# Strassen products of the first layer: from the first halves of batches 3, 5 and 7 to four tiles of batch 1

## The chip, the cores and the metric

The kernel runs on one core of a Trainium2 chip. The core has a matrix engine (TensorE, PE), a vector engine (VectorE, DVE), a scalar engine (ScalarE, ACT), a general engine (GpSimd, POOL), and a queue engine (SyncE, SP) that issues most of the transfers. They share an on-chip memory (SBUF); PE writes its results into a small accumulator memory (PSUM), from which DVE and ACT read. The metric is the device time of one execution in microseconds (us). The kernel before has a median of 765.96 us over three runs (765.54 to 766.06).

## What is computed

An attention block that reads a small state, followed by a two-layer network whose weights are shared by all tokens:

```python
def _attn_ref(x, state):                      # x: 8 x 8 x 512 x 64, state: 8 x 8 x 32 x 64
    scale = 1.0 / np.sqrt(D)
    scores = scale * np.matmul(x, state.transpose(0, 1, 3, 2))
    a = softmax(scores)
    xread = np.matmul(a, state)
    scores2 = scale * np.matmul(state, x.transpose(0, 1, 3, 2))
    a2 = softmax(scores2)
    sread = np.matmul(a2, x)
    return np.concatenate([xread, sread], axis=2)

def _moe_ref(x, w_in, w_out):                 # x: 4352 x 512, d_ff 2048
    h = x @ w_in
    g = h * np.cos(h)
    return g @ w_out
```

(`softmax` stands here for the three lines of the reference that subtract the maximum, exponentiate and divide by the sum.) There are 8 batches of 512 token rows and 32 state rows. All is computed in float32; the weights arrive as float64 and are converted on the chip.

## The kernel before

**The first layer through the state.** A token's row is a mean of state rows with attention weights, so the kernel doesn't form the row. It multiplies the state with `w_in` once for each batch (`products`, kept in `sw`), and then the attention weights `aT` (256 of them for each token, in two groups of 128 partitions) with `sw`. A batch has 2048 hidden columns, worked on as 16 *tiles* of 128 columns by 512 tokens. A *plain* tile is two matmuls of 512 columns into a PSUM buffer (`hidden`, line 471). There are two such buffers (`hps`), used in turn.

**Strassen couples.** For some tiles, two neighbouring tiles are computed together: a 2 x 2 block product (two groups of state rows by two tiles, two groups by two halves of the tokens) with 7 half-width products in place of 8. `hidden_a` issues four of the products (L514), `hidden_b` three. They need:
- four differences of the attention weights for each batch (`halves`, L493, on DVE, kept in `aS`);
- four sums of 128 x 128 blocks of `sw` for each couple (`sw_sums`, L509): on POOL, except that line 506 puts them on DVE where `t.b < 2 or t.b == 2 and t.f == 0`;
- an ACT copy of one product to SBUF (L536), and five sums on DVE (`sums_a`: L544, L545, L546; `sums_b`: L559, L560) that make the two tiles in `g_all`, in SBUF, before the gate.

Where a plain tile stands directly ahead of a Strassen couple, its result is first copied out of PSUM by ACT (L957), since the couple takes both PSUM buffers.

**The gate.** `h cos h` is four operations for each tile: ACT rounds (L567, `gate`), DVE subtracts (L570, `gate2`), ACT takes the sine (L573, `gate3`), DVE multiplies (L580, `gate4`). For a plain tile L570 and L580 read `h` in PSUM; for a tile of a couple they read it in SBUF, in `g_all`.

**The second layer by Strassen.** Batches are paired (0 and 1, 2 and 3, ...). A pair's 32 tiles go through four phases of 8 tiles. In phases 2 and 3 (the odd batch) differences of gated tiles are formed (`minus`, L586): on POOL, except that in the later pairs one for each tile is on DVE. Products of the second layer (L624) follow three steps behind the tile; two of the seven products of a pair are done in the next pair's steps (`more`).

**The order.** The schedule is written out by hand, and each engine runs its queue in that order. A *step* is one tile; step 16 b + f is tile f of batch b. `plan` spreads the attention of the next batch over the steps: DVE transposes (L301), scores on PE (L319), maxima, exponentials on ACT, sums and norms (L333 to L386). During batches 0 and 1 the weights are also converted (L228, L231 on ACT, L234, L237 on DVE, L242 on POOL, up to step 16), and at steps 16 to 22, and 32 and 33, POOL forms the sums of blocks of `w_out` that the second layer's Strassen needs (`blocks`, L912). Within a step the order is: the step's first-layer matmuls and, ahead of a couple, that couple's first four products; attention on PE; gate and subtraction; the couple's sums; attention on DVE; the sine; a store; state sums for a couple two steps on; the product; `minus`; attention again; differences of attention weights for a couple five steps on; POOL's block sums; the second layer's matmuls.

**Which tiles are in couples.** `seven(t)` on line 480 decides. Before, these are all 16 tiles of batches 2, 4 and 6 (phases 0 and 1) and the first 8 of batches 3, 5 and 7 (phase 2). `halves` of an odd batch is issued in the last couple of the even one, that of an even batch five steps ahead of it (L1009).

Of the kernel before, what the change touches and what calls it, by code (L numbers as in the profile page):

```python
# [21 lines left out]
def kernel(  # L22
# [44 lines left out]
    NH = NF // 2  # L67
# [75 lines left out]
    def states(half, to):  # L143
        for i in range(4):
            nc.tensor.transpose(out=to[:, P * i:P * i + P],
                                in_=st[:, 4 * half + i, :], identity=ident)
# [36 lines left out]
    def fetch(n):  # L183
        nonlocal n_fetched
        while n_fetched < n:
            dst, src = loads[n_fetched]
            if f64:
                m, w = dst.shape[1:]

                at_, c0 = (n_fetched - 2) % 3, 0  # L190
                if n_fetched < 4:
                    at_, c0 = n_fetched // 2, n_fetched % 2 * 2 * m * w
                if n_fetched >= N_LOADS:
                    at_ = 3 + n_fetched - N_LOADS
                raw = raw_at[at_].bitcast(I32)[:, c0:c0 + 2 * m * w]
                raw = raw.rearrange("p (m f) -> p m f", m=m)
                nc.sync.dma_start(out=raw, in_=src.bitcast(I32))
                raws[n_fetched] = raw.rearrange("p m (f w) -> p m f w", w=2)
            else:
                nc.sync.dma_start(out=dst, in_=src)  # L200
            n_fetched += 1
# [6 lines left out]
    def convert(i, parts):  # L208

        for p in parts:
            if p == "f":
                if i not in (1, 2) and i + 3 < N_LOADS:
                    fetch(max(i + 4, 6))
            elif f64:
                convert_part(i, p)
# [234 lines left out]
    def part(b, name, *args):  # L453

        if b not in attn:
            attn[b] = Attention(b)
        getattr(attn[b], name)(*args)
        if (name, args) == ("reads", (1,)) and b + 1 < B:
            if b > 0:
                attn[b + 1] = Attention(b + 1)  # L460
                attn[b + 1].load_tokens()
            load_x(b + 1)
# [5 lines left out]
    def hidden(t):  # L468
        t.hp = hps.tile([P, S], F32, name="h")[:, 0:t.n]
        for i in range(t.kn):  # L470
            nc.tensor.matmul(out=t.hp, lhsT=t.lhs(i), rhs=t.rhs(i),  # L471
                             start=(i == 0), stop=(i == t.kn - 1))
# [4 lines left out]


    def seven(t):
        return t.pair is not None and t.b > 1 and t.phase < 3  # L480

    def new_pair(t):
        return t.b % 2 == 0 and t.f == 0

    def halves(b):
        aT = aT_of[b]
        b11, b12 = aT[:, 0, 0:HS], aT[:, 0, HS:S]
        b21, b22 = aT[:, 1, 0:HS], aT[:, 1, HS:S]  # L490
        for i, x1, x2 in ((0, b12, b11), (1, b22, aS[:, 0]), (2, b22, b12),
                          (3, b21, aS[:, 1])):
            nc.vector.tensor_tensor(aS[:, i], x1, x2, op=ALU.subtract)  # L493
# [22 lines left out]
    def take_slot(t):  # L516
        t.slot = g_free.pop(0)
        t.hp = t.g = g_all[:, t.slot, 0:t.n]
# [7 lines left out]
    def hidden_a(t, t2):  # L526
        b11, b12, b21, b22 = blocks_of(t)
        t.h1, t.h2 = [hps.tile([P, S], F32, name="h") for _ in range(2)]
        product_of(t.h1[:, LO], b11, aT_of[t.b][:, 0, LO])
        product_of(t.h1[:, HI], swS[:, 1], aS[:, 1])  # L530
        product_of(t.h2[:, HI], b21, aS[:, 2])
        product_of(t.h2[:, LO], swS[:, 0], aS[:, 0])
        take_slot(t)
        take_slot(t2)
        t.second = t2
        nc.scalar.copy(t.g[:, LO], t.h1[:, LO])  # L536
# [12 lines left out]
    def hidden_b(t):  # L549
        b11, b12, b21, b22 = blocks_of(t)  # L550
        t.h1, t.h2 = [hps.tile([P, S], F32, name="h") for _ in range(2)]
        product_of(t.h1[:, LO], b12, aT_of[t.b][:, 1, LO])
        product_of(t.h2[:, HI], swS[:, 2], aT_of[t.b][:, 1, HI])
        product_of(t.h2[:, LO], b22, aS[:, 3])

    def sums_b(t):
        e, o = 2 * t.slot, 2 * t.second.slot
        add = nc.vector.tensor_tensor
        add(t.g[:, LO], t.g[:, LO], t.h1[:, LO], op=ALU.add)  # L559
        add(both(o, e + 1), both(o, e + 1),  # L560
            t.h2.rearrange("p (h s) -> p h s", h=2), op=ALU.add)
# [3 lines left out]
    def gate(t):  # L565
        t.q = msb.tile([P, S], F32, name="q")[:, 0:t.n]
        nc.scalar.activation(t.q.bitcast(I32), t.hp, func=ACTF.Copy, bias=0.25)  # L567

    def gate2(t):
        nc.vector.tensor_tensor(t.q, t.q.bitcast(I32), t.hp, op=ALU.subtract)  # L570

    def gate3(t):
        nc.scalar.activation(t.q, t.q, func=ACTF.Sin, bias=halfpi,  # L573
                             scale=-TWO_PI)

    def gate4(t):
        if not hasattr(t, "slot"):
            t.slot = g_free.pop(0)
            t.g = g_all[:, t.slot, 0:t.n]
        nc.vector.tensor_tensor(t.g, t.hp, t.q, op=ALU.mult)  # L580
# [217 lines left out]
    def warm(n, to):  # L798

        for _ in range(n):  # L800
            nc.tensor.matmul(out=to, lhsT=zeros[:, 0:P], rhs=zeros, start=True,
                             stop=True)
# [124 lines left out]
    for step, t in enumerate(all_tiles):  # L927
        s = step % NF
        if s == 0 and t.b < B:
            steps = plan(t.b)  # L930
        todo = [p[s] if t.b < B else [] for p in steps]

        def go(n):
            for p in todo[n]:
                part(*p)

        last, conv = conv_at.get(step - 1, -1), conv_at.get(step, -1)
        if step == B * NF + (0 if f64 else 8):
            fetch(N_LOADS + 2)
        if step == 4:  # L940
            warm(1, acc[MAIN][0])
        ahead = all_tiles[step + 1:step + 3]
        if seven(t):
            if t.f % 2 == 0:
                hidden_b(t)
                sums_b(t)
                if s == NF - 2 and seven(all_tiles[step + 2]):
                    halves(t.b + 1)
        elif step != 1:
            hidden(t)  # L950
        first = len(ahead) > 1 and seven(ahead[0]) and ahead[0].f % 2 == 0
        if first:
            if not seven(t):

                h = t.hp
                take_slot(t)
                nc.scalar.copy(t.g, h)  # L957
            hidden_a(*ahead)
        if step == 0:
            hidden(all_tiles[1])  # L960
            warm(3, acc[MAIN][0])
            gate(t)
            gate2(t)
            convert(3, "bcdf")
            convert(4, "1")
            go(0)
        else:
            go(0)
            if step == 5:
                states(1, acc[SIDE][1])  # L970
            if not (seven(t) and t.f % 2):
                gate(t)
            gate2(t)
            if step == 3:
                warm(4, acc[MAIN][0])
                part(0, "products", 1, SIDE)
            if first:
                sums_a(ahead[0])
            go(1)
            go(3)  # L980
            if step == 1:
                convert(4, "bcdf")
            elif last >= 0:
                convert(last, "bcdf")
            if conv >= 0 and not todo[1]:
                convert(conv, "1")
        gate3(t)
        if seven(t) and t.f % 2 == 0:
            gate(t.second)
        if step == 3:  # L990
            part(0, "products_kept", 1, SIDE)
        if later:
            later.pop(0)()
        for u, new in zip(all_tiles[step + 2:step + 4], (False, True)):
            if seven(u) and u.f % 2 == 0 and new_pair(u) == new:
                sw_sums(u)
        gate4(t)
        if conv >= 0 and todo[1] and step > 0:
            convert(conv, "1")
        if t.pair is not None:  # L1000
            sums(t)
        if step == 6:
            states_kept(1, acc[SIDE][1])
        go(2)
        if conv >= 0:
            convert(conv, "2")
        go(4)
        for u in all_tiles[step + 5:step + 6]:
            if seven(u) and new_pair(u):  # L1009
                halves(u.b)  # L1010
        if step in block_at:
            blocks(*block_at[step])
        if t.pair is not None:
            sums2(t)
        while len(line) >= (LAG if step >= 2 * NH else LAG + 1):
            output(line.pop(0))
        line.append(t)
# [32 lines left out]
```

## Time and profile before

| what | value |
|---|---|
| median of three runs | 765.96 us |
| the profiled execution | 765.96 us |
| its span, first to last instruction | 764.2 us |
| granted PE clock | 0.997 |
| PE busy | 751.7 us, 2880 records |
| DVE busy | 520.3 us, 862 instructions |
| ACT busy | 316.3 us, 523 instructions |
| POOL busy | 249.3 us, 258 instructions |
| PE busy, 0 to 75 us | 68.64 us |
| PE busy, 75 to 160 us | 85.00 us |
| PE busy, 160 to 764 us | 598.09 us |
| DVE busy, 94 to 131 us (batch 0's last steps and the first half of batch 1) | 29.26 of 37 us |
| POOL busy, 94 to 131 us | 28.44 of 37 us |

A float32 matmul shows as two records. A group's mean is the length of one record from its start to its modelled end; successive records overlap, so the distance from one start to the next is what a record adds to PE's time. In rows of the timeline the columns are the start, the length, the engine, the line, the operation, what is written and read, the shape, the count, and in brackets the idle time ahead of it with what ended it. Busy time doesn't tell whether an operation was working or held up: where another engine stands in its way inside the operation, the row is simply longer than others of its form.

In the built program the tiles of batch 1 begin at 97.48 us (step 16) and step 24 begins at 130.43; the first couple of batch 2 is issued at 168.89.

### The profile page before, as it was taken

To read this page: it belongs to the slowest core of one execution; us is meant where nothing else is said; L and a number is where in the kernel's file an instruction comes from. 1 tells how busy PE (TensorE), PEld (TensorE's weight loads), DVE (VectorE), ACT (ScalarE), POOL (GpSimd) and SP (SyncE) were. 2 spreads that over 40 slices of the span, in tenths; PEclk is the share of its full clock that TensorE was granted. 3 is DMA by queue.
4 is the path that set the end of the run, shared out by engine and by line. 5 is a ranking of instruction groups with operands and counts; after the bars stand their busy time and mean duration, and the time that the engine had idled before them with its cause. 6 is when DMAs were issued, how large, how long until landed. Compare 5 with 4: busy or idle time off the path is not lost.

```text
span 764.2 us, 8416 instructions
## 1 busy us (share of the span) xinstructions
PE 751.7 (98%) x2880; PEld 380.4 (50%) x2880; DVE 520.3 (68%) x862; ACT 316.3 (41%) x523; POOL 249.3 (33%) x258
## 2 busy tenths in 40 slices
PE   8998999999999999999999999999999999999997
PEld 3443443445555554445555553445555554455554
DVE  5778777836896788847886789747878676432431
ACT  3887844533254335333362335333443333212212
POOL 2354278777121210662221111751211206500200
PEclk9999999999999999999999999999999999999999
DMA  8595461050002510340105210420100115000021
GB/s 247 170 274 209 131 98 29 4 107 1 14 15 49 90 28 4 54 82 0 29 1 97 41 28 15 70 54 1 27 1 1 28 28 138 0 0 15 14 42 41
DMA packets 161962, 43.54 MB, mean 57 GB/s; under 512 B 153920, under 2 KB 153920, under 8 KB 161920
## 3 DMA queue, kind: packets, MB, share of 16 engines
q1 hardware_dynamic: 161024, 42.49, 25.7%
q10 hardware_dynamic: 768, 0.39, 0.2%
q8 instruction: 23, 0.38, 0.2%
q14 instruction: 19, 0.16, 0.1%
q0 software_dynamic: 128, 0.13, 0.1%
HBM read 34.08 MB, written 8.91 MB: 56 GB/s over the span
## 4 chain that ended last, share of the span: by engine, by line
PE 87%; DVE 7%; ACT 2%; issue 1%; DMA 1%; POOL 1%; SPq 0%; DVEq 0%; ACTq 0%; POOLq 0%
PE o L624 47%; PE h L514 14%; PE h L471 14%; PE at L319 4%; PE o L744 4%; PE at L409 2%; DVE xT L339 1%; PE o L319 1%; DVE q L570 1%; DVE g_all L580 1%; DVE i L333 1%; DMA g_all<-in_moe_w_in_dram 1%; ACT q L567 1%; PE at L392 1%; DVE aT L356 1%
## 5 line engine op out<-in xcount | busy, mean ns | idle before, releaser
L624 PE MATMUL o<-g_all,w_out 128*128 128x512 f32 x512 | 236.4, 598 | 0.4 <-POOL w_out L242 0.4
L624 PE MATMUL o<-g_all,s 128*128 128x512 f32 x384 | 177.3, 598 | 0.0
L586 POOL TENSOR_TENSOR g_all<-g_all 128x512 f32<-128x512 f32 x80 | 112.8, 1433 | 121.2 <-DVE g_all L580 121.2
L624 PEld LDWEIGHTS o<-g_all,w_out 128*128 128x128 f32 x512 | 93.8, 190 | 113.1 <-issue 108.4
L573 ACT ACTIVATE q<-q,halfpi 128x512 f32<-128x512 f32 (+1 forms) x144 | 100.8, 700 | 95.8 <-DVE q L570 95.6
L624 PEld LDWEIGHTS o<-g_all,s 128*128 128x128 f32 x384 | 70.8, 190 | 88.1 <-issue 82.1
L570 DVE TENSOR_TENSOR q<-q,h 128x512 f32<-128x512 int32 (+1 forms) x69 | 42.9, 621 | 103.6 <-ACT q L567 103.6
L471 PE MATMUL h<-aT,sw 128*128 128x512 f32 x224 | 107.2, 602 | 4.8 <-DVE g_all L580 4.3
L567 ACT ACTIVATE q<-g_all 128x512 int32<-128x512 f32 x75 | 46.8, 624 | 141.8 <-DVE g_all L560 141.4
L567 ACT ACTIVATE q<-h 128x512 int32<-128x512 f32 (+1 forms) x69 | 37.6, 545 | 131.0 <-PE h L471 131.0
L570 DVE TENSOR_TENSOR q<-q,g_all 128x512 f32<-128x512 int32 x75 | 52.7, 703 | 35.5 <-ACT q L567 35.5
L471 PEld LDWEIGHTS h<-aT,sw 128*128 128x128 f32 x224 | 41.8, 190 | 60.2 <-issue 45.0
L509 POOL TENSOR_TENSOR swS<-sw 128x128 f32<-128x128 f32 x35 | 17.4, 496 | 148.6 <-PE h L514 107.3
L580 DVE TENSOR_TENSOR g_all<-g_all,q 128x512 f32<-128x512 f32 x75 | 54.0, 720 | 14.5 <-ACT q L573 14.4
L580 DVE TENSOR_TENSOR g_all<-h,q 128x512 f32<-128x512 f32 (+1 forms) x69 | 42.8, 621 | 23.5 <-ACT q L573 23.1
L242 POOL TENSOR_TENSOR w_out<-w_out,s 128x1024 int32<-128x1024 int32 x10 | 23.9, 2390 | 77.6 <-DVE w_out L237 73.4
L509 POOL TENSOR_TENSOR swS<-sw,swS 128x128 f32<-128x128 f32 x35 | 18.3, 522 | 87.4 <-PE h L514 86.9
L514 PEld LDWEIGHTS h<-aT,sw 128*128 128x128 f32 x144 | 27.4, 190 | 34.4 <-issue 28.0
L514 PE MATMUL h<-aS,sw 128*128 128x256 f32 x144 | 43.1, 381 | 0.1
L514 PE MATMUL h<-aS,swS 128*128 128x256 f32 x144 | 42.8, 379 | 0.0
L514 PE MATMUL h<-aT,sw 128*128 128x256 f32 x144 | 42.8, 379 | 0.0
L586 DVE TENSOR_TENSOR g_all<-g_all 128x512 f32<-128x512 f32 x48 | 33.5, 697 | 1.6
(107 smaller groups left out, 886.3 us busy)
## 6 DMA issues: line engine op xcount, KB each, us to landing
out_dram<-ot SPq DMA_DIRECT2D x132, 64.0 KB, 2.0
g_all<-in_moe_w_out_dram SPq DMA_DIRECT2D x8, 1024.0 KB, 5.0
g_all<-in_moe_w_in_dram SPq DMA_DIRECT2D x6, 1024.0 KB, 5.3
xT<-in_x_dram SPq DMA_DIRECT2D x96, 64.0 KB, 2.3
x_b<-in_x_dram SPq DMA_DIRECT2D x24, 256.0 KB, 4.5
x_b<-in_x_dram SPq DMA_DIRECT2D x16, 128.0 KB, 3.8
g_all<-in_moe_w_in_dram SPq DMA_DIRECT2D x4, 512.0 KB, 5.9
x_b<-in_moe_w_out_dram SPq DMA_DIRECT2D x1, 1024.0 KB, 6.1
```

The lines of the kernel that those rows point to most:

```text
L242: nc.gpsimd.tensor_tensor(bits, bits, e, op=ALU.add)
L319: nc.tensor.matmul(out=(to or at)[j][Ns * k:Ns * k + Ns, 0:n], lhsT=w[D * j:D * j + D, self.b, Ns * k:Ns * k + Ns], rhs=r(slice(D * j, D * ...
L471: nc.tensor.matmul(out=t.hp, lhsT=t.lhs(i), rhs=t.rhs(i), start=(i == 0), stop=(i == t.kn - 1))
L509: engine.tensor_tensor(o, x1, x2, op=op)
L514: nc.tensor.matmul(out=out, lhsT=w, rhs=r, start=True, stop=True)
L567: nc.scalar.activation(t.q.bitcast(I32), t.hp, func=ACTF.Copy, bias=0.25)
L570: nc.vector.tensor_tensor(t.q, t.q.bitcast(I32), t.hp, op=ALU.subtract)
L573: nc.scalar.activation(t.q, t.q, func=ACTF.Sin, bias=halfpi, scale=-TWO_PI)
L580: nc.vector.tensor_tensor(t.g, t.hp, t.q, op=ALU.mult)
L586: engine.tensor_tensor(out, a, b, op=ALU.subtract)
L624: nc.tensor.matmul(out=acc[bank][ch], lhsT=w[:, i, P * ch:P * ch + P], rhs=g.g, start=(i == 0), stop=(i == NH - 1))
L744: nc.tensor.matmul(out=acc[MAIN][i], lhsT=t.g[:, P * i:P * i + P], rhs=w_out[:, :, t.f, :], start=(t.n_th == 0), stop=(t.n_th == NF - 1))
```

## The change

`seven` takes another set of tiles: tiles 4 to 7 of batch 1 (two couples) come in, and the first halves of batches 3, 5 and 7 (12 couples) go out and are plain again. Batches 2, 4 and 6 stay. The second edit issues `halves(1)` five steps ahead of tile 4 of batch 1, that is at step 15; the `halves` of batches 3, 5 and 7 are no longer issued.

```diff
     def seven(t):
-        return t.pair is not None and t.b > 1 and t.phase < 3
+        if t.b == 1:
+            return 4 <= t.f < NH
+        return t.pair is not None and t.b > 1 and t.phase < 2
@@
         for u in all_tiles[step + 5:step + 6]:
-            if seven(u) and new_pair(u):
+            if seven(u) and new_pair(u) or (u.b, u.f) == (1, 4):
                 halves(u.b)
```

What follows from it in the queues, with the lines as they are numbered before: the couples of batch 1 are tiles 20 and 21, and 22 and 23. `hidden_a` of the first is issued in step 19, behind the plain tile 19, whose result ACT copies out (L957); `hidden_a` of the second in step 21. Their state sums are issued in steps 18 and 20 ahead of that step's product (L580), on DVE by line 506, which is as it was. In the built programs PE has 40 full-width matmuls more (L471) and 70 half-width ones fewer (L514); DVE has 8 fewer L493, 8 more L509 and 50 fewer of the couples' sums; ACT has 10 fewer L536 and one more L957; POOL has 48 fewer L509. 19 tiles more have their L567, L570 and L580 read PSUM. SP's queue is the same in both.

## The prediction

> **What bounds the kernel now.** I read the page first (busy shares, then the chain that ended last), then that chain in order of time, then the timelines of TensorE (PE), VectorE (DVE), ScalarE (ACT) and GpSimd (POOL) over the steps that change. From the page, shares of the span, the chain and three groups:
>
> ```profile
> PE 751.7 (98%) x2880; PEld 380.4 (50%) x2880; DVE 520.3 (68%) x862; ACT 316.3 (41%) x523; POOL 249.3 (33%) x258
> PE 87%; DVE 7%; ACT 2%; issue 1%; DMA 1%; POOL 1%; SPq 0%; DVEq 0%; ACTq 0%; POOLq 0%
> L471 PE MATMUL h<-aT,sw 128*128 128x512 f32 x224 | 107.2, 602 | 4.8 <-DVE g_all L580 4.3
> L514 PE MATMUL h<-aS,sw 128*128 128x256 f32 x144 | 43.1, 381 | 0.1
> L586 POOL TENSOR_TENSOR g_all<-g_all 128x512 f32<-128x512 f32 x80 | 112.8, 1433 | 121.2 <-DVE g_all L580 121.2
> ```
>
> PE is busy 98% and carries 87% of the chain, so its arithmetic is the time, unless another engine makes it wait. The means in the groups (602, 381 ns) overlap, so I price a record by the chain in order of time (start, length, number of records):
>
> ```profile
> 334.84 1.72 PE h L471 x4
> 187.13 3.43 PE o L624 x8
> 190.57 1.73 PE h L514 x8
> ```
>
> A 512-column record costs 1.72/4 = 0.43 us, a 256-column one 1.73/8 = 0.216. Every matmul is two records.
>
> **PE's arithmetic.** A couple of plain tiles is 4 matmuls, 8 records at 0.429 = 3.43 us. A Strassen couple is 7 half-width matmuls, 14 records at 0.216 = 3.02. The difference is 0.41. The change makes 12 couples plain (batches 3, 5, 7: +4.9 us) and 2 Strassen (batch 1: -0.8 us). In the built order of the changed kernel the counts agree: 40 more full matmuls, 70 fewer half ones. The change is also said to put batch 2's first state sums on DVE; that moves nothing: line 506 puts them on DVE in both kernels, and the old trace has them there (four L509 rows from 159.75).
>
> **What leaves batches 3, 5 and 7.** 12 couples lose five DVE sums (L544 to L560, 0.41 to 0.69 us each, 2.6 us a couple), 12 L493 differences, an ACT copy a couple, and POOL's 48 sums of state products. In 249 to 297 us PE has no idle time (48.00 busy of 48.00), so none of that gains anything there. Behind it, at the start of the plain half, PE does wait:
>
> ```profile
> 304.95 1.98 PE L471 MATMUL h<-aT,sw 128*128 128x512 f32 x4 [0.18 <-DVE g_all L580]
> 310.32 1.98 PE L471 MATMUL h<-aT,sw 128*128 128x512 f32 x4 [0.79 <-DVE g_all L580]
> ```
>
> From start to start these are 0.35 and 0.95 us lost, in batches 3 and 5 (the rows repeat at 472 to 478; batch 7 prepares no next batch). The cause is a late queue: the exponentials on ACT start after step 7's gates, whose DVE part stands behind the sums of the last couple. Without them gate 55 comes some 1.2 to 1.5 us earlier. The gain lies between 0 and 2 x 1.3 = 2.6; I take 2.0. Plain tiles hold their PSUM buffer through the whole gate, 4.8 us from the first matmul, and a buffer is wanted again after two steps, at least 2 x 3.43 us, so I price no new wait there. No DMA is moved.
>
> **Batch 1.** Here DVE gets 4 differences (L493) at step 15, twice 4 state sums (L509) at steps 18 and 20, and twice 5 sums. What they cost depends on POOL. From DVE's timeline, the same four differences before batch 2 (POOL running) and, last line, one before batch 3 (POOL idle); start, length:
>
> ```profile
> 147.68 0.81 DVE L493 TENSOR_TENSOR aS<-aT 128x256 f32<-128x256 f32 x1
> 148.52 1.37 DVE L493 TENSOR_TENSOR aS<-aT,aS 128x256 f32<-128x256 f32 x1
> 149.81 1.49 DVE L493 TENSOR_TENSOR aS<-aT 128x256 f32<-128x256 f32 x1
> 151.22 1.49 DVE L493 TENSOR_TENSOR aS<-aT,aS 128x256 f32<-128x256 f32 x1
> 250.58 0.42 DVE L493 TENSOR_TENSOR aS<-aT 128x256 f32<-128x256 f32 x1
> ```
>
> Each waits for the POOL operation in progress (16.5 us of L586 back to back from 138.56), runs, and lets the next POOL operation go. The same holds for a gate that reads two SBUF operands (L580 at 184.23: 1.89 us instead of 0.69), and not for one that reads PSUM. So the four tiles' gates, which read PSUM now and SBUF then, come under it as well. And POOL is full in these steps:
>
> ```profile
> 106.86 1.26 POOL L586 TENSOR_TENSOR g_all<-g_all 128x512 f32<-128x512 f32 x1
> 108.09 2.35 POOL L912 TENSOR_TENSOR s<-w_out 128x1024 f32<-128x1024 f32 x1
> 110.40 1.27 POOL L586 TENSOR_TENSOR g_all<-g_all 128x512 f32<-128x512 f32 x1
> 113.54 2.37 POOL L912 TENSOR_TENSOR s<-w_out 128x1024 f32<-128x1024 f32 x1
> ```
>
> I walk the queues in their built order with the distances of a plain tile (step 18: matmul 107.39, gate 109.37, subtraction 110.00, sine 110.72, product 111.48; product to reuse of its PSUM buffer 0.70, from 304.25 and 304.95; product to POOL's L586 0.83, from 111.48 and 112.31). PE before, for comparison:
>
> ```profile
> 107.39 1.88 PE L471 MATMUL h<-aT,sw 128*128 128x512 f32 x4
> 110.83 1.88 PE L471 MATMUL h<-aT,sw 128*128 128x512 f32 x4
> 112.54 1.88 PE L624 MATMUL o<-g_all,s 128*128 128x512 f32 x4
> ```
>
> 1. Step 15: the differences stand behind the product of 100.00. POOL's conversion (100.22, 2.37 us) holds the first until 102.6; all end at 103.9. Behind them on DVE: gate 16, two copies, a conversion (together 3.6 us), product 16 at 107.5 (before 104.51). The matmuls of tile 18 want its buffer: 108.2 instead of 107.39, **0.8 lost**.
> 2. Step 18: the four state sums stand ahead of product 18. They are ready at 112.05; POOL is in L912 until 113.75, then in L586 until 115.25; they end at 115.85 instead of 113.05. Product 18 at 115.85; the first Strassen product wants its buffer at 113.4 and gets it at 116.55: **3.15 lost**.
> 3. Step 19: ACT's gate now stands behind two copies (L957, L536): 117.9. Its subtraction meets L912 (118.0 to 120.35). The couple's sums run from 120.85 to 122.5, and the second three products want those two buffers: **2.1 lost**.
> 4. Step 20: subtraction 20 meets L912 until 128.2; behind it two copies, a transposition, then the second four state sums, ready at 131.05. The first product of couple 22 has gone at 126.1, its second waits: **4.6 lost**.
> 5. Steps 21 to 24: products 21, 22 and 23 come at 136.2, 142.3 and 147.4 (before 123.35, 127.94, 132.25), each behind another L912. PE isn't stopped, having outputs and free buffers, until tile 26 wants the buffer of product 24, which comes at 152.5 instead of 137.80. Tile 26 starts at 153.2 instead of 138.51: **14.7 us** in all, the 0.8 saved already in it. From there on steps are longer (4.4 to 6.4 us) and nothing gives this back.
>
> Two unknowns. No row shows a 128x128 DVE sum beside a running POOL operation. If it does not wait, item 2 falls from 3.15 to about 0.4; if each of the four waits out a POOL operation as L493 does (1.45 each), item 2 grows by 2. I take the row it is nearest to, L493. And some waits hang on who comes first: subtraction 22 meets L912 by 0.2 us, subtraction 19 by 0.5; if both slip ahead, 4 us go. [...]
>
> **Sum.** Span 764.2 + 4.9 - 2.0 + 14.7 = 781.8; the profiled execution took 765.96 with 1.8 around its span, and 765.96 is also the median. So **783.5 us**. This case's own range is 776 to 789.
>
> **Rivals.**
> - *No lock in batch 1.* The same walk with each operation at its bare length: nothing lost at step 15, 0.4 at step 19, 0.35 at 20, 3.05 at the second state sums, and product 23 at 137.1 instead of 132.25, so tile 26 is 4.85 late. 764.2 + 4.9 - 2.0 + 4.85 + 1.8 = **773.7**. For it: POOL has gaps of 0.65 to 0.99 us between 111 and 129. Against: L493 and L580 above.
> - *Arithmetic only.* DVE is busy 29.3 of 37 us from 94 to 131; if the 10 us of added work fitted in, PE alone would tell: 765.96 + 4.9 - 0.8 - 2.0 = **768.1**. Against: 29.3 + 10 is over 37.
> - *Faster.* Taking some 30 us off DVE and the sums off POOL frees PE of waits in general. Place: PE's 12.5 us of idle time (764.2 - 751.7). It decides from 4.1 us on, what the arithmetic costs; at half of 12.5 the time is 765.96 + 4.1 - 6.25 = **763.8**. Against: 6.4 of the 12.5 lie in the first 75 us, which the change doesn't touch, none from 75 to 160, and 4.0 behind the last product (which ends at 753.30 + 6.88); 2.0 to 2.6 is all that is left for it.
>
> **Chances.** Forecast 0.68, no lock 0.16, arithmetic only 0.11, faster 0.03, within 0.02. 0.2% (1.5 us) is about what can be told from no change here; so faster 0.03, same 0.02, slower 0.95. The range 769 to 788 takes in the no-lock case and nearly all of the forecast's own; it leaves out arithmetic only, faster, no change and the far end, some 0.19 together.
>
> **What would show it.** L471 has 304 records of 512 columns instead of 224, L514 364 instead of 504. PE is idle between 107 and 154 us, in waits on L580, L546 and L509; the four L493 at about 100 us take over 2 us together; L570 and L580 on SBUF take over 1 us beside L912. Batches 3, 5 and 7 each grow by 1.6 us of PE time, and the two waits at the start of their plain halves shrink. If PE shows no idle time in batch 1, the walk is wrong; if it does but beside DVE operations at their bare length, the lock is.

## The result, and the profile after

The changed kernel takes 783.44 us (median; 782.38 to 785.01) against 765.75 for the kernel before in the same set: a ratio of 1.0235, 95% interval 1.0211 to 1.0258. It is 17.7 us slower; 783.5 was forecast. The profiled execution took 782.38 us, its span is 780.6. From the page of the changed kernel: busy time, the chain by engine, and two groups of first-layer matmuls (behind the bar: busy time and mean, idle time ahead and what ended it):

```profile
PE 757.8 (97%) x2820; PEld 369.7 (47%) x2820; DVE 505.7 (65%) x812; ACT 315.0 (40%) x514; POOL 227.3 (29%) x210
PE 86%; DVE 7%; ACT 2%; SPq 1%; DMA 1%; issue 1%; POOL 1%; DVEq 0%; ACTq 0%; POOLq 0%
L471 PE MATMUL h<-aT,sw 128*128 128x512 f32 x304 | 143.4, 595 | 8.2 <-DVE g_all L582 7.6
L516 PE MATMUL h<-aS,swS 128*128 128x256 f32 x104 | 32.1, 391 | 4.2 <-DVE swS L511 4.2
```

(Below line 481 the changed kernel's numbers are 2 higher: L582 is the product L580, L572 the subtraction L570, L546 to L562 the couples' sums, L511 the state sums, L495 the differences, L516 the half-width matmuls, L588 POOL's `minus`, L914 its block sums.)

DVE and POOL do less than before in total (505.7 against 520.3 us, 227.3 against 249.3) and the kernel is slower. PE got more work, and it now waits for a DVE that is less busy over the span. Where it waits is a matter of place. Three marks on PE split the span:

| stretch | before | after | difference |
|---|---|---|---|
| start to the first matmul of step 16 | 97.48 | 96.25 | -1.2 |
| step 16 to the first couple of batch 2 | 71.40 | 87.09 | +15.7 |
| that couple to the last product | 590.69 | 592.63 | +1.9 |

The last product starts 4.6 us ahead of the span's end in both. The first stretch has the same instructions in both; the profiled executions of the kernels below that leave it alone put step 16 anywhere from 96.0 to 97.6, so single executions are compared from step 16 on.

PE in batch 1, from its timeline (start, length, line, what is written and read, records, idle time ahead and what ended it):

```profile
108.21 1.98 PE L471 MATMUL h<-aT,sw 128*128 128x512 f32 x4 [1.78 <-DVE g_all L582]
114.30 0.70 PE L516 MATMUL h<-aT,sw 128*128 128x256 f32 x2 [0.68 <-ACT g_all L959]
116.01 0.70 PE L516 MATMUL h<-aS,sw 128*128 128x256 f32 x2 [0.43 <-DVE g_all L582]
120.70 0.67 PE L516 MATMUL h<-aT,sw 128*128 128x256 f32 x2 [1.84 <-DVE g_all L546]
130.57 1.22 PE L516 MATMUL h<-aS,swS 128*128 128x256 f32 x2 [4.16 <-DVE swS L511]
131.59 1.06 PE L516 MATMUL h<-aS,sw 128*128 128x256 f32 x2
152.95 1.98 PE L471 MATMUL h<-aT,sw 128*128 128x512 f32 x4 [3.50 <-DVE g_all L582]
```

None of these waits is in the kernel before. The DVE rows that make DVE late for them:

```profile
100.32 2.25 DVE L495 TENSOR_TENSOR aS<-aT 128x256 f32<-128x256 f32 x1
102.61 0.42 DVE L495 TENSOR_TENSOR aS<-aT,aS 128x256 f32<-128x256 f32 x1
112.15 1.40 DVE L511 TENSOR_TENSOR swS<-sw 128x128 f32<-128x128 f32 x1
113.59 1.24 DVE L511 TENSOR_TENSOR swS<-swS,sw 128x128 f32<-128x128 f32 x1
114.86 0.29 DVE L511 TENSOR_TENSOR swS<-sw,swS 128x128 f32<-128x128 f32 x1
117.67 2.56 DVE L572 TENSOR_TENSOR q<-q,g_all 128x512 f32<-128x512 int32 x1
125.81 2.39 DVE L572 TENSOR_TENSOR q<-q,g_all 128x512 f32<-128x512 int32 x1 [0.70 <-ACT q L569]
```

and POOL at the same time:

```profile
99.94 2.35 POOL L242 TENSOR_TENSOR w_out<-w_out,s 128x1024 int32<-128x1024 int32 x1 [1.95 <-ACT st_all L430]
111.05 2.36 POOL L914 TENSOR_TENSOR s<-w_out 128x1024 f32<-128x1024 f32 x1
113.37 1.31 POOL L588 TENSOR_TENSOR g_all<-g_all 128x512 f32<-128x512 f32 x1
117.33 2.35 POOL L914 TENSOR_TENSOR s<-w_out 128x1024 f32<-128x1024 f32 x1
125.31 2.34 POOL L914 TENSOR_TENSOR s<-s,w_out 128x1024 f32<-128x1024 f32 x1
```

Read across: the first difference starts at 100.32 and ends at 102.57; POOL's conversion ends at 102.29 (99.94 + 2.35). Its bare length is 0.42, as in the next row. The subtraction at 117.67 lasts 2.56 instead of 0.69; POOL's L914 ends at 119.68. The first two state sums end just behind POOL's 113.41 and 114.68, the third meets nothing and takes 0.29. Each long row ends behind the end of a POOL row by its bare length less some 0.14 us, so it waits for the end of the operation on POOL and then runs: 0.28 of 0.42, 0.14 and 0.15 of 0.29, 0.55 of 0.69.

### The profile page after: what moved, and what is told of

The parts are those of the page before. It is cut to its first block, busy times and chain, and to the rows that moved or that the text cites. A ratio compares the mean times of both kernels' runs of the same rounds, so it can differ in the third digit from the quotient of the medians.

```text
span 780.6 us, 8148 instructions
## 1 busy us (share of the span) xinstructions
PE 757.8 (97%) x2820; PEld 369.7 (47%) x2820; DVE 505.7 (65%) x812; ACT 315.0 (40%) x514; POOL 227.3 (29%) x210
## 4 chain that ended last, share of the span: by engine, by line
PE 86%; DVE 7%; ACT 2%; SPq 1%; DMA 1%; issue 1%; POOL 1%; DVEq 0%; ACTq 0%; POOLq 0%
PE o L626 47%; PE h L471 18%; PE h L516 10%; PE at L319 4%; PE o L746 4%; PE at L409 2%; DVE q L572 1%; SPq L292 1%; PE at L392 1%; DVE g_all L582 1%; ACT q L569 1%; DMA x_b<-in_x_dram 1%; PE o L319 0%; DVE i L333 0%; DVE w_out L237 0%
## 5 line engine op out<-in xcount | busy, mean ns | idle before, releaser
L588 POOL TENSOR_TENSOR g_all<-g_all 128x512 f32<-128x512 f32 x80 | 113.2, 1437 | 254.7 <-DVE g_all L582 250.6
L471 PE MATMUL h<-aT,sw 128*128 128x512 f32 x304 | 143.4, 595 | 8.2 <-DVE g_all L582 7.6
L572 DVE TENSOR_TENSOR q<-q,h 128x512 f32<-128x512 int32 (+1 forms) x88 | 56.0, 637 | 141.5 <-ACT q L569 141.5
L569 ACT ACTIVATE q<-h 128x512 int32<-128x512 f32 (+1 forms) x88 | 49.1, 557 | 188.7 <-PE h L471 188.5
L471 PEld LDWEIGHTS h<-aT,sw 128*128 128x128 f32 x304 | 57.0, 190 | 81.9 <-issue 62.2
L582 DVE TENSOR_TENSOR g_all<-h,q 128x512 f32<-128x512 f32 (+1 forms) x88 | 55.9, 636 | 33.3 <-ACT q L575 32.9
L569 ACT ACTIVATE q<-g_all 128x512 int32<-128x512 f32 x56 | 34.9, 623 | 100.2 <-DVE g_all L562 99.8
L572 DVE TENSOR_TENSOR q<-q,g_all 128x512 f32<-128x512 int32 x56 | 44.9, 802 | 30.1 <-ACT q L569 30.1
L582 DVE TENSOR_TENSOR g_all<-g_all,q 128x512 f32<-128x512 f32 x56 | 40.2, 717 | 10.4 <-ACT q L575 10.3
L516 PE MATMUL h<-aS,swS 128*128 128x256 f32 x104 | 32.1, 391 | 4.2 <-DVE swS L511 4.2
L511 POOL TENSOR_TENSOR swS<-sw 128x128 f32<-128x128 f32 x23 | 11.4, 495 | 83.1 <-PE h L516 65.9
L588 DVE TENSOR_TENSOR g_all<-g_all 128x512 f32<-128x512 f32 x48 | 33.5, 697 | 1.6
L516 PE MATMUL h<-aT,sw 128*128 128x256 f32 x104 | 31.1, 381 | 2.5 <-DVE g_all L546 1.8
L516 PEld LDWEIGHTS h<-aT,sw 128*128 128x128 f32 x104 | 19.6, 190 | 28.1 <-issue 22.3
L516 PE MATMUL h<-aS,sw 128*128 128x256 f32 x104 | 31.7, 387 | 0.6 <-DVE g_all L582 0.4
L445 ACT COPY sw<-at 128x512 f32<-128x512 f32 x50 | 26.7, 586 | 10.4 <-PE at L319 10.0
```

The lines of the kernel that those rows point to most:

```text
L445: (copy or nc.scalar.copy)(sw_of[self.b, nt][:, j, c0:c1], to[j][:, 0:c1 - c0])
L471: nc.tensor.matmul(out=t.hp, lhsT=t.lhs(i), rhs=t.rhs(i), start=(i == 0), stop=(i == t.kn - 1))
L516: nc.tensor.matmul(out=out, lhsT=w, rhs=r, start=True, stop=True)
L588: engine.tensor_tensor(out, a, b, op=ALU.subtract)
```

## The experiments

**Each half alone.** First the odd halves plain and nothing in batch 1:

```diff
-        if t.b == 1:
-            return 4 <= t.f < NH
         return t.pair is not None and t.b > 1 and t.phase < 2
@@
-            if seven(u) and new_pair(u) or (u.b, u.f) == (1, 4):
+            if seven(u) and new_pair(u):
```

> Only one half of the change: the first halves of batches 3, 5 and 7 are plain, and batch 1 stays plain too. My theory: 12 couples at 0.41 us more PE time are 4.9 us, the two waits at 304 and 309 us and their repeats in batch 5 (2.6 us) go, so about 2.3 us over the kernel before (768.0 beside 765.75), with no wait of TensorE in batch 1. Rival: the plain tiles hold PSUM through the whole gate and bring waits of their own in batches 3, 5 and 7; then 771 or more.

Measured: 767.33 us against 766.19, ratio 1.0015 (1.0005 to 1.0025): 1.1 us slower, 0.4 to 1.9. No wait in batch 1: from step 16 to the first couple of batch 2 it takes 71.50 us, as before (71.40). From that couple to the last product it takes 592.62, 1.93 more than before. Both are under the 2.3 expected, which lies outside the interval. The parts show why. From the first couple of batch 6 to the last product, where four couples became plain and there was no wait to lose, it takes 257.54 us instead of 255.89: 1.65 more, as priced. Each of the two stretches ahead of it, with batch 3 and with batch 5, grew by only 0.14, where 1.65 - 1.3 = 0.35 was expected. The missing 0.2 are in the rows behind the two waits: from their start to the next row they take 1.72 and 1.81 us here (306.33 to 308.05, 310.64 to 312.45), and took 1.82 and 1.91 behind the waits. The rival is out.

Then the couples in batch 1 with the odd halves as before:

```diff
-        return t.pair is not None and t.b > 1 and t.phase < 2
+        return t.pair is not None and t.b > 1 and t.phase < 3
```

> Only the other half: tiles 4 to 7 of batch 1 in couples, batches 3, 5 and 7 as before. My theory: batch 1 alone costs 14 to 16 us (780 to 782), and the two parts add up to the whole. Rival: the parts help or hurt one another, through queues that run on into batch 2; then this one lies more than 2 us off 781.

Measured: 782.07 us, ratio 1.0206 (1.0186 to 1.0226), 15.9 slower. Behind batch 2's first couple it takes 590.69, to 0.01 us what the kernel before takes. So the parts don't touch one another: 15.9 + 1.1 = 17.0 against 17.7 for the whole, within the intervals.

One difference in this execution matters later. PE's waits in batch 1 are those of the changed kernel to 0.01 us, but from step 16 to batch 2 it takes 88.61 us instead of 87.09. It comes from the rows behind the wait at tile 26 (PE, granted clock 0.62 from 153.5 to 158 us; 1.00 from 152.9 to 159 in the changed kernel's execution):

```profile
152.59 2.51 PE L471 MATMUL h<-aT,sw 128*128 128x512 f32 x4 [3.49 <-DVE g_all L582]
154.89 1.92 PE L392 MATMUL at<-ident,xT 128*128 128x128 f32 x8
```

The changed kernel's four runs stand at 782.38 and 782.40 with a mean granted clock of 0.997, and at 784.49 and 785.01 with 0.993. The profiled one is of the first kind.

**Is it the GpSimd operation in progress that DVE waits for?** The block sums in quarters:

```diff
-        nc.gpsimd.tensor_tensor(out_[:, r], a[:, r], b[:, r], op=op)
+        n = (r.stop - r.start) // 4
+        for i in range(r.start, r.stop, n):
+            q = slice(i, i + n)
+            nc.gpsimd.tensor_tensor(out_[:, q], a[:, q], b[:, q], op=op)
```

> The changed kernel with each of GpSimd's block sums (L912 of the kernel before, 2.36 us each) issued as four operations of a quarter of the columns: same work, same place in the queue, same data. My theory (a DVE operation with two SBUF operands waits for the GpSimd operation in progress to end): its waits beside the block sums, 1.9, 1.7 and 1.05 us on the subtractions and 1.1 on a state sum, fall to at most 0.6 each, and the time by 3 to 5 us to 778 to 780. Rival (the queue of DVE is simply too long at the operations' bare lengths, or both engines share bandwidth): within 1 us of 783.4.

Measured: 780.02 us, ratio 1.0185 (1.0157 to 1.0214), so 3.4 us under the changed kernel's median; the two intervals overlap at their ends. The rows leave less doubt. From the timelines of this kernel, the subtractions of tiles 19 and 20 and then POOL beside the first (L917, four pieces in a row, merged):

```profile
118.96 0.93 DVE L572 TENSOR_TENSOR q<-q,g_all 128x512 f32<-128x512 int32 x1
125.48 1.11 DVE L572 TENSOR_TENSOR q<-q,g_all 128x512 f32<-128x512 int32 x1 [0.70 <-ACT q L569]
```

```profile
118.62 3.23 POOL L917 TENSOR_TENSOR s<-w_out 128x256 f32<-128x256 f32 x4
```

The same subtractions, in the same place, take 0.93 and 1.11 us instead of 2.56 and 2.39. POOL's work is no less (four pieces take 2.8 to 3.8 us instead of 2.36), so it isn't a matter of how much POOL does but of how long one of its operations is. One part of the expectation failed: the four state sums of step 18 take 3.21 us together, as in the changed kernel. Now each of them waits for a piece (0.46, 0.70, 0.70), and the last, 1.35 us, waits for POOL's `minus` (115.18, 1.31 us). All of the gain lies behind them: tile 26 comes 54.18 us behind step 16 instead of 56.70. In the profiled execution, the slowest of the four runs, 1.7 of these 2.5 us were lost again, because the rows behind tile 26's wait ran at a granted clock of 0.57 (from 152 to 156 us).

**Do TensorE's waits add up, or does DVE's queue set the end?** The second couple's state sums one step earlier, into a free slot of `g_all`:

```diff
+    swS2 = g_all[:, NG - 1, 0:3 * P].rearrange("p (i m) -> p i m", i=3)
@@
-            if seven(u) and u.f % 2 == 0 and new_pair(u) == new:
+            if seven(u) and u.f % 2 == 0 and new_pair(u) == new and (
+                    u.b, u.f) != (1, 6):
                 sw_sums(u)
+        if step == 19:
+            sw_sums(all_tiles[22])
```

(the couple's sums and products then use `swS2`)

> The changed kernel with the state sums of couple 22 issued one step earlier (ahead of product 19 instead of product 20), into a place of their own. TensorE's longest wait in batch 1 (4.3 us, before the second product of couple 22) should go. Rival: TensorE's waits add up, so the time falls by what that wait costs, 4.3 us and the slow records behind it, some 6 us to 777.5. My theory: the waits only show DVE's late queue, which stays as long; the wait moves to the next place where TensorE wants a buffer, and the time falls by 1 to 2 us, to 781 to 782.5.

Measured: 783.97 us, ratio 1.0228 (1.0207 to 1.0248): no gain. From PE's timeline of this kernel, the second product of couple 22 and the first of tile 26 (L520 is the half-width matmul here, L586 the gate's product):

```profile
127.92 0.59 PE L520 MATMUL h<-aS,g_all 128*128 128x256 f32 x2
152.40 3.78 PE L472 MATMUL h<-aT,sw 128*128 128x512 f32 x4 [5.71 <-DVE g_all L586]
```

The wait of 4.16 us is gone, and the one at tile 26 has grown from 3.50 to 5.71: tile 26 starts at 152.40 instead of 152.95. The wait moved, as the theory says, but the gain of 1 to 2 us that I expected did not come. DVE was ahead by 1.3 us at the product of tile 21 (135.07 instead of 136.23, in an execution 0.1 later at step 16), but then the subtraction of tile 22 met the block sum earlier in its run and took 2.58 us instead of 1.74. What was left, some 0.6 us, was lost in the next rows: four records in 3.78 us, twice the usual 1.88 (granted clock 0.50 from 152 to 156 us). That is the next experiment's subject.

**The slow records.** Four extra matmuls, whose result nobody reads, in the wait before couple 22's second product, into a PSUM bank that is free there:

```diff
         product_of(t.h1[:, LO], b11, aT_of[t.b][:, 0, LO])
+        if (t.b, t.f) == (1, 6):
+            for _ in range(4):
+                nc.tensor.matmul(out=at[0], lhsT=b11, rhs=aT_of[t.b][:, 0],
+                                 start=True, stop=True)
         product_of(t.h1[:, HI], swS[:, 1], aS[:, 1])
```

> The changed kernel with four matmuls of 512 columns, whose result nobody reads, issued behind the first product of couple 22, in TensorE's wait of 4.3 us. If the slow records behind that wait (0.43 us each instead of 0.216, granted clock 0.57 from 130 to 134 us) come from TensorE having been idle, they are 0.216 here. Theory on the time: DVE's queue sets when tile 26 starts, so it stays within 1 us of 783.4. Rival: slow records on the path cost their 1.8 us, and the time falls to 781.6.

Measured: 783.43 us, ratio 1.0236 (1.0221 to 1.0252), the changed kernel's own time. From 130 to 134 us, the row by stretch (busy time of PE, weight loads, DVE, ACT and POOL with their counts, granted clock, share of the DMA engines, GB/s), first of the changed kernel, then of this one:

```profile
130.00:134.00 4.00, 3.43 (x14) 2.08 (x22) 3.01 (x10) 1.09 (x2) 2.22 (x2) 0.57 0.41 66
```

```profile
130.00:134.00 4.00, 4.00 (x26) 1.82 (x26) 3.73 (x10) 1.09 (x2) 2.36 (x2) 1.00 0.43 68
```

The granted clock goes from 0.57 to 1.00, and the records behind the wait from 0.43 to 0.216 us each: they were slow because PE had been idle. The time stayed, as expected, but not for the reason given alone. The slow records had held DVE up too: in the changed kernel a sum of couple 22 waits for them (first row, DVE), here it doesn't, and tile 26 comes 0.6 us sooner, 56.06 us behind step 16 instead of 56.70. Then its own rows ran slowly (second row, PE; granted clock 0.61 from 152.1 to 156.5), and from step 16 to batch 2 it takes 88.13 us instead of 87.09:

```profile
133.54 0.42 DVE L547 TENSOR_TENSOR g_all<-g_all,h 128x256 f32<-128x256 f32 x1 [0.88 <-PE h L516]
152.17 2.91 PE L471 MATMUL h<-aT,sw 128*128 128x512 f32 x4 [3.86 <-DVE g_all L586]
```

So the half clock at 130 us costs some 0.6 us of the time, since DVE's queue hides the rest, while behind tile 26 PE has no such slack and loses all of it, some 1.7 us (from tile 26's start to L409 7.91 us instead of 6.23).

**What is the step 15 part worth?** The four differences at step 12:

```diff
-            if seven(u) and new_pair(u) or (u.b, u.f) == (1, 4):
+            if seven(u) and new_pair(u) or (u.b, u.f) == (1, 1):
```

> The changed kernel with the four differences of attention weights of batch 1 (L493 of the kernel before) issued at step 12 instead of 15, where GpSimd has nothing running. Theory: they cost their bare 1.4 us there, hidden; DVE's queue is not late at step 16, the wait of tile 18 (0.8 us against the kernel before, 1.95 in the changed one's profile) goes, the state sums at step 18 are ready earlier, and tile 26 starts 2 to 3 us earlier: 780.5 to 781.5. Rival: DVE has slack before step 18 and step 15 costs nothing in the end: 783.4.

Measured: 782.00 us, ratio 1.0212 (1.0193 to 1.0230), some 1.4 us under the changed kernel, with overlapping intervals. That lies between the theory and the rival. My ground was wrong: GpSimd was idle during step 12 in the kernel before, but the differences come at its end, and meet the next conversion. From DVE's and POOL's timelines:

```profile
86.04 2.27 DVE L495 TENSOR_TENSOR aS<-aT 128x256 f32<-128x256 f32 x1
```

```profile
85.67 2.37 POOL L242 TENSOR_TENSOR w_out<-w_out,s 128x1024 int32<-128x1024 int32 x1 [10.56 <-ACT w_out L228]
```

So the price moved: PE loses 1.84 us just ahead of step 16, which starts at 97.94, and nothing at tile 18. From step 16 tile 26 comes after 53.20 us instead of 56.70, and batch 2 after 85.15 instead of 87.09; between the two, this execution ran at half clock (0.53 from 151 to 154.5 us) where the changed kernel's didn't. So the step 15 differences cost 2 to 3.5 us there, 1.84 of which came back ahead of step 16: they have no free place at step 12 either.

**The two waits behind the odd halves.** From the kernel before, with the last couple of batches 3 and 5 plain:

```diff
-        return t.pair is not None and t.b > 1 and t.phase < 3
+        return t.pair is not None and t.b > 1 and t.phase < 3 and (
+            t.b not in (3, 5) or t.f < 6)
```

> The kernel before with one couple fewer in batches 3 and 5 (tiles 6 and 7 plain; batch 7 as before; batch 1 plain). Theory: the two waits behind these halves (0.35 and 0.95 us, in both batches) come from the last couple's sums, which stand ahead of step 7's gates on DVE; without it they go for 2 x 0.41 us more TensorE time: 0.8 - 2.6, so 1.8 us faster than the kernel before. Rival: DVE's queue is late from the earlier couples on, the waits stay, and it is 0.8 us slower.

and with the last two (`t.f < 4`):

> The same with two couples fewer in batches 3 and 5 (tiles 4 to 7 plain). Theory: the waits go here too, for 1.6 us of TensorE time: 1.0 us faster than the kernel before, 0.8 slower than with one couple fewer. Rival: if the waits need both couples gone, this one is 1.0 us faster and the other 0.8 slower.

Measured: one couple fewer 763.51 us against 766.08, ratio 0.9971 (0.9962 to 0.9980); two fewer 765.28, ratio 0.9995 (0.9987 to 1.0004), not to be told from no change. The first is faster than both kernels of this study, by 2.2 us (1.5 to 2.9) against the one before, where 1.8 was expected. From PE's timeline of it, the tiles that waited:

```profile
305.11 1.88 PE L471 MATMUL h<-aT,sw 128*128 128x512 f32 x4
309.42 1.88 PE L471 MATMUL h<-aT,sw 128*128 128x512 f32 x4
```

Neither has idle time ahead of it now, and PE has no such wait in batch 5 either. With two fewer both waits go as well, but in batches 3 and 5 another comes, 0.65 us each from start to start, ahead of products of the second layer at 273.60 and 440.96. They wait for DVE's L631, and take what was to remain of the gain:

```profile
273.60 1.98 PE L625 MATMUL o<-g_all,s 128*128 128x512 f32 x4 [0.48 <-DVE held L631]
```

## Why the prediction was right, point by point

- *PE's arithmetic* (+4.9 and -0.8 us): the counts are those of the built order, 304 and 364 records (104 + 104 + 104 + 52 of L516). Batch 7 alone shows the price: four couples made plain cost 1.65 us.
- *The relief behind the odd halves*: taken as 2.0, bounded by 2.6. The stretch from batch 2 on grew by 1.9, so 4.9 - 1.9 = 3.0 were given back, more than my upper bound. The mechanism is shown by the kernel with one couple fewer; the size was off because I took less than the two waits, where both vanished whole, and because the rows behind each wait were 0.1 us slow, 0.4 us in all.
- *The walk through batch 1*: 14.7 predicted, 15.7 found from step 16 on. The profiled execution reached step 16 1.2 us early, but DVE's product of step 15 only 0.3 us early (99.72 instead of 100.00). From there on DVE's queue was late and no longer followed PE, so the head start was worth nothing, and the walk's readings are compared directly:

| event | predicted | measured |
|---|---|---|
| product 16 starts | 107.5 | 107.46 |
| tile 18 starts | 108.2 | 108.21 |
| product 18 starts | 115.85 | 115.27 |
| subtraction 19 starts, held by L912 | yes, at 118.5 | yes, at 117.67 |
| second product of couple 22 | 131.05 | 130.57 |
| products 21, 22, 23 come at | 136.2, 142.3, 147.4 | 136.23, 142.24, 147.00 |
| tile 26 starts | 153.2 | 152.95 |

- *What held products 21 to 23*: the walk put each behind a block sum. Product 22 was (the subtraction ahead of it took 1.74 us beside L914), and product 23 too, though behind an operation that the walk had not counted: L351, a DVE `tensor_scalar` on 128x2 elements in SBUF, took 1.01 us instead of 0.17 and ended with the block sum. Product 21 came on time for another reason: DVE waited 0.88 and 0.32 us for PE ahead of it, whose records were slow. That its time fits is a coincidence.
- *Item 2 was mis-sized for PE*: 3.15 us lost were predicted at the first couple, 1.8 were (5.23 us from tile 19's first matmul at 111.75 to the product behind the couple at 116.98, where the records need 3.44). The couple's first two products waited for ACT's copy of tile 19 and the last two for product 18, the other way round than I had assumed from batch 2, so half of the couple ran ahead of the late product. It cost the sum nothing: PE then lost more at item 3 (2.9 instead of 2.1: 6.00 us from 116.98 to 122.98, where the records need 3.1), because DVE's queue, not the sum of PE's waits, sets tile 26. The early state sums show this most plainly.
- *The unknowns*: a 128x128 sum beside a running POOL operation does wait (1.40 and 1.24 us instead of 0.29), as the rows of L493 beside POOL suggested (0.81 to 1.49 us instead of 0.42). The close calls at subtractions 19 and 22 went the expensive way.
- *Unforeseen*: the half clock behind PE's waits (0.57 from 130 to 134 us, records of 0.43 us instead of 0.216). It cost PE some 1.6 us at 130 us, of which DVE's queue hid all but some 0.6. Behind tile 26 it cost the time 1.6 to 2.3 us in the five profiled executions that have it; the changed kernel's profiled one doesn't.
- *Luck*: the total came out within 0.2 us (17.5 forecast, 17.7 measured) because two misses cancel: from step 16 batch 1 lost 1.0 us more than the walk gave, and the odd halves cost 1.0 less than 4.9 - 2.0. The walk had no term for the clock.
- *The rivals*: "no lock" is refuted by the long rows beside POOL and by the quarters, "arithmetic only" and "faster" by PE's 12 us of waits between 107 and 153 us (40.61 us busy of 53 from 107 to 160).

## What to carry to other kernels

Before moving work to an engine with spare time over the span, look at that stretch of its queue: here DVE was 68% busy, and 29.26 of 37 us in the stretch, which had no room for some 9 us more (4 differences, 8 state sums and 10 couple sums at their bare lengths). Price an operation that reads two SBUF operands on DVE by its own length plus what is left of the GpSimd operation then in progress (here a subtraction of 0.69 us, begun 2.01 us ahead of the end of a block sum, took 2.56), and try cutting long GpSimd operations into pieces where such operations must pass: here that brought about 3 us. And follow the queue that is late to its last consumer: removing one visible wait of another engine moved it on here (4.16 us went, and the next wait grew from 3.50 to 5.71).

## What the runs showed of the hardware

PE's granted clock fell to 0.52 to 0.62, read over 3 to 4.5 us, behind waits of 1.85 to 4.16 us, and not behind all of them. In the changed kernel it was 0.57 from 130 to 134 us, behind 4.16 us of waiting, and stayed at 1.00 from 152 to 156, behind 3.50. The kernel with batch 1's couples alone has the same wait there, 3.49 us, and its clock fell, to 0.62 from 153.5 to 158. With the block sums in quarters it was 0.52 from 128 to 132 behind 2.88 us, and 0.57 from 152 to 156 behind 2.61. In the kernel with the extra matmuls, but ahead of them, it was 0.53 from 122.5 to 126, behind two waits of 1.85 and 0.58, where the changed kernel had 1.00 from 120.7 to 124 behind the same two. In the kernel before, a single wait of 1.95 us, with 1.00 and no idle time from 67 to 71 us ahead of it, is followed by 0.61 from 73 to 76.2. A slow phase lasted some 3 us there, and some 6 in the kernel with the quarters, where the records are long from 128.96 to about 135. The length of a wait alone doesn't tell the clock behind it (3.50 and 3.49 us, 1.00 and 0.62); what decides was not shown.
